# Gate arithmetic for two query chunks at a time in a fused attention and expert kernel

## The chip, the cores and the metric

The kernel runs on one core of one Trainium2 chip. The metric is the device time of one execution in microseconds (us). A core has five engines with queues of their own: TensorE (PE, matmul; its weight loads are PEld), VectorE (DVE), ScalarE (ACT), GpSimd (POOL) and SyncE (SP, which here only issues loads). Each runs its instructions in the order of the program and stops at an instruction whose input is not ready.

## The reference, cut to what matters

```python
# attention: B=4, N=11456, C=128, 49 agents
agent_v = softmax(scale * agents @ k.T) @ v
x = softmax(scale * q @ agents.T) @ agent_v          # (4*11456, 128)
# mixture of experts: 8 experts, D=128, F=1024
do_compute = x @ w_skip > 0
logits = x[do_compute] @ w_gate
e_idx = argmax(logits, axis=1)
gate_w = softmax(logits)[e_idx]
y = gate_w * (relu(x @ w1[e_idx]) @ w2[e_idx])
out = x;  out[do_compute] += y
```

## The kernel before, in words

A batch of 11456 tokens is 90 columns of 128 tokens (the last column is half full). Columns are taken in chunks of 6, so a batch is 15 chunks (`ci` 0 to 14) and the run has 60 of them (n = 15 b + ci). The program is written out in 101 slots. In each slot a table, `ORDER`, names the stages, and each stage takes the chunk that is its lag behind. A stage's name is its letter and its step: k for keys (`sK` scores, `kS` store and running maximum), v for values (`vS` shift, `vE` exp, `vA` product), q and the rest for queries (`sQ` scores, `qS` maximum, `qE` exp, `qT` transpose, `mX` product with the agents' values and the gate matrix, `qN` division, `qD` gate weight, `qG` gate exp, `qO` output). The order in which they are named is the order on every engine:

```python
"kvq": "qN+4 qD+5 sQ+1 bg vE qS+1 sK qE+1 vS-1 qG+4 kS qT+2 bg rt vA qO+5 mX+3 rt wt"
"vq": "qN+4 qD+5 sQ+1 bg vE qS+1 qE+1 vS-1 qG+4 bg qT+2 rt vA qO+5 mX+3 rt wt"
"q": "qN+4 qD+5 sQ+1 qS+1 qE+1 qG+4 bg qT+2 rt qO+5 rt mX+3 rt wt"
```

Keys, values and queries all flow in the slots from 33 to 59 (kvq), values and queries in 60 to 77 (vq), queries alone after that (q). Below, a slot is named by the chunk that `qN` divides in it: "slot n16" begins with the division of chunk 16, whose first instruction is L438 on DVE. So kvq covers n0 to n23, vq n24 to n41, q n42 to n59.

`qN` (L433) reads the product in PSUM (`px`, a single buffer, so the next `mX` waits until both L446 divisions are done), writes the output rows `xs` and the nine gate numbers `G` (eight logits and the skip score), and takes the maximum of the logits, `top` (L460). `qG` subtracts it on POOL (L467) and takes the exp on ACT (L469). `qD`, a slot later, sums (L475) and inverts (L476), which gives the gate weight, and `qO` sends the chunk out from the ACT queue.

Two words move work that belongs to no chunk. `rt` takes one step, up to the next `yield`, of the oldest generator in a queue. These are `codes` (L486: the index of the winning expert, for four chunks at a time, from `G == top`, and its one-hot `mask`), `ranks` (L532) and `routing` (L543), which turn the masks of a batch into each token's place in its expert's list. `mask` and its running counts `cum` come in two parts, of 72 columns (part 0) and 18 columns (part 1). Part 0's place is mask*cum, summed over experts (`sel`, L541), plus mask*start, summed over experts (`acc`, L598), added at L613. `bg` steps the rest: `agent_values` and `early` (L643), which finds the tokens of the first two expert blocks while attention still runs.

When the attention is over, `experts` runs blocks of 384 tokens through w1 and w2, with queues written by hand; the change leaves it as it is.

Of the kernel before, what the change touches and what calls it, by code (L numbers as in the profile page):

```python
# [52 lines left out]
PAR = dict(v=3, q=-1, cols=6, ld=8, more=5, qe=3, eT=2, xs=3, tail=3, early=-8,  # L53
# [74 lines left out]
def attention(nc, tc, sh, io, ps):  # L128
# [10 lines left out]
    with ExitStack() as ctx:  # L139
# [346 lines left out]
        def codes(first, last):  # L486
# [6 lines left out]
            hot = dict(out=best, in0=g[:, :, :NE], in1=top[:, first:last].unsqueeze(2).to_broadcast([P, m, NE]),  # L493
                       op=ALU.is_equal)
            order = dict(out=best, in0=best, in1=desc.unsqueeze(1).to_broadcast([P, m, NE]), op=ALU.mult)
            found = dict(out=mask[i][:, :, first - i * NA_ : last - i * NA_],
                         in0=c.unsqueeze(1).to_broadcast([P, NE, m]),
                         in1=cidx.unsqueeze(2).to_broadcast([P, NE, m]), op=ALU.is_equal)
            if i == 0:
                vec.tensor_tensor(**hot)  # L500
                pool.tensor_tensor(**order)
                yield
                vec.tensor_reduce(c, best, axis=AX.X, op=ALU.max)
                yield
                vec.scalar_tensor_tensor(out=c, in0=g[:, :, NE], scalar=0.0, in1=c, op0=ALU.is_gt, op1=ALU.mult)
                vec.tensor_tensor(**found)
            else:
                vec.tensor_tensor(**hot)
                vec.tensor_tensor(**order)
                vec.tensor_reduce(c, best, axis=AX.X, op=ALU.max)  # L510
                yield
                vec.scalar_tensor_tensor(out=c, in0=g[:, :, NE], scalar=0.0, in1=c, op0=ALU.is_gt, op1=ALU.mult)
                vec.tensor_tensor(**found)
# [29 lines left out]
        def routing(b):  # L543
# [644 lines left out]
```

## Time and profile before

| | |
|---|---|
| median of 3 runs | 786.96 us (785.77 to 787.64) |
| profiled execution: its time, its span | 788.92 us, 787.2 us |
| busy over the span: PE, PEld, DVE, ACT, POOL | 708.2 (90%), 665.6 (85%), 513.3 (65%), 377.2 (48%), 384.1 us (49%) |
| mean granted clock of TensorE | 0.954 of full speed |
| attention ends, first expert matmul begins | 384.4 us, 386.9 us |

The span runs from the first instruction to the last; the time has 1.7 us more around it. Busy times are sums over engines that work side by side, so they add up to more than the span. What limits the kernel changes from stretch to stretch, and the shares above are means over all of them.

### The profile page before, as it was taken

What the parts mean: (1) busy time and instruction counts of PE and PEld (TensorE: products, weight loads), DVE (VectorE), ACT (ScalarE), POOL (GpSimd) and SP (SyncE); (2) the same over time, 40 slices, a digit from 0 to 9 for tenths busy, and PEclk for the clock granted to TensorE, in tenths of its full rate; (3) what the DMA queues carried; (4) which work ended last, traced back from release to release, by engine and by line L of the source; (5) the groups of instructions that cost most, each with busy time, mean ns of one, the idle gap of its engine ahead of it and who ended that gap; (6) DMA issues with size and microseconds to landing.
All of it is one profiled execution on the core that took longest, in us unless ns stands there. A gap on an engine that the chain in (4) does not pass through costs nothing. (4 is left out here: it accounts for less than half of the span.)

```text
span 787.2 us, 18201 instructions
## 1 busy us (share of the span) xinstructions
PE 708.2 (90%) x5542; PEld 665.6 (85%) x5542; DVE 513.3 (65%) x1776; ACT 377.2 (48%) x1076; POOL 384.1 (49%) x482
## 2 busy tenths in 40 slices
PE   6999999989798878884399969999999999999994
PEld 6988999878677767774399969999999999999994
DVE  3424456675667878977667656766767767777663
ACT  3444554444334535553155535555555555555552
POOL 4554233232323251441366663666666666666665
PEclk9999999999889989897599999999999999999998
DMA  9999899988679837653111110111111111111110
GB/s 317 393 387 372 265 371 347 329 263 300 238 223 294 270 101 255 234 183 123 30 36 46 39 30 21 36 49 48 46 49 49 46 51 45 45 47 47 49 28 20
DMA packets 65673, 120.47 MB, mean 153 GB/s; under 512 B 21126, under 2 KB 29322, under 8 KB 65616
## 3 DMA queue, kind: packets, MB, share of 16 engines
q1 hardware_dynamic: 48192, 81.34, 31.6%
q10 hardware_dynamic: 9456, 23.89, 7.7%
q0 software_dynamic: 7968, 14.54, 6.6%
q8 instruction: 29, 0.48, 0.2%
q14 instruction: 28, 0.23, 0.1%
HBM read 87.78 MB, written 31.90 MB: 152 GB/s over the span
## 5 line engine op out<-in xcount | busy, mean ns | idle before, releaser
L946 DVE SCALAR_TENSOR_TENSOR hl<-h,hh 128x384 fp32r<-128x384 f32 x320 | 165.1, 551 | 72.8 <-DVEq L835 72.8
L1008 ACT ACTIVATE hh<-h 128x384 fp32r<-128x384 f32 x320 | 157.1, 492 | 115.1 <-ACTq L835 110.0
L1036 POOL DMA_INDIRECT xg<-out_dram,ids x123 | 125.8, 1023 | 110.1 <-issue 109.8
L409 ACT ACTIVATE qe<-ps_s,qm 128x49 f32<-128x49 f32 x360 | 76.1, 312 | 151.4 <-DVE qm L403 151.4
L1049 POOL DMA_INDIRECT out_dram<-xo,sid x123 | 122.6, 997 | 37.5 <-issue 36.9
L1107 PE MATMUL h<-xh,w 128*128 128x384 f32 x512 | 132.1, 340 | 7.5 <-PEq L835 7.5
L1113 PE MATMUL y<-hh,w 128*128 128x384 f32 x512 | 135.9, 347 | 0.0
L316 PE MATMUL ps_s<-agT,ld 128*128 128x128 f32 x960 | 128.9, 291 | 6.3 <-ACT agT L168 6.3
L316 PEld LDWEIGHTS ps_s<-agT,ld 128*128 128x128 f32 x960 | 118.1, 201 | 17.1 <-ACT agT L168 6.3
L1107 PEld LDWEIGHTS h<-xh,w 128*128 128x128 f32 x512 | 93.2, 190 | 8.2 <-issue 8.1
L1113 PEld LDWEIGHTS y<-hh,w 128*128 128x128 f32 x512 | 88.5, 188 | 1.3 <-issue 0.2
L1107 PE MATMUL h<-xl,w 128*128 128x384 f32 x256 | 86.8, 339 | 0.0
L1113 PE MATMUL y<-hl,w 128*128 128x384 f32 x256 | 86.3, 337 | 0.0
L332 DVE TENSOR_TENSOR run<-scores,run 128x294 f32<-128x294 f32 x56 | 28.7, 513 | 85.0 <-ACT scores L327 83.2
L430 PE MATMUL ps_x<-av,eT 50*128 50x138 f32 x720 | 62.4, 307 | 19.6 <-DVE G L446 16.8
L467 POOL TENSOR_TENSOR ex<-G,top 128x48 f32<-128x48 f32 x60 | 16.3, 271 | 125.1 <-DVE gs L475 68.8
L430 PEld LDWEIGHTS ps_x<-av,eT 50*128 50x128 f32 x720 | 49.9, 196 | 31.4 <-issue 22.0
L316 PE MATMUL ps_s<-agT,lds 128*128 128x128 f32 x480 | 65.1, 292 | 0.0
L316 PEld LDWEIGHTS ps_s<-agT,lds 128*128 128x128 f32 x480 | 60.2, 203 | 5.6 <-issue 3.9
L446 DVE TENSOR_TENSOR xs<-ps_x,qr 128x768 f32<-128x768 f32 x60 | 57.5, 959 | 6.5 <-DMA out_dram<-xs 4.3
L1004 ACT ACTIVATE yT<-y 128x384 f32<-128x384 f32 x40 | 19.7, 492 | 65.3 <-ACTq L835 65.3
L920 DVE SCALAR_TENSOR_TENSOR junk<-id,rs,jot 128x90 f32<-128x90 f32 x120 | 31.1, 308 | 28.0 <-DVEq L835 28.0
(193 smaller groups left out, 1168.7 us busy)
## 6 DMA issues: line engine op xcount, KB each, us to landing
out_dram<-xs ACTq DMA_DIRECT2D x60, 387.0 KB, 4.7
ld<-in_q_dram SPq DMA_DIRECT2D x44, 384.0 KB, 4.7
ld<-in_v_dram SPq DMA_DIRECT2D x38, 387.0 KB, 5.6
ld<-in_k_dram SPq DMA_DIRECT2D x36, 384.0 KB, 5.7
lds<-in_k_dram SPq DMA_DIRECT2D x24, 384.0 KB, 6.3
lds<-in_v_dram SPq DMA_DIRECT2D x22, 387.0 KB, 5.3
ld<-in_moe_w_dram SPq DMA_DIRECT2D x24, 256.0 KB, 5.6
lds<-in_q_dram SPq DMA_DIRECT2D x16, 384.0 KB, 5.6
```

Source lines behind the costliest of these rows:

```text
L316: r.append(ten.matmul(pt[:, t * NA : t * NA + P], lhsT=xT[:, t * P : (t + 1) * P], rhs=agT[:, b, :], start=True, stop=True))
L332: vec.tensor_tensor(out=run, in0=stored(n), in1=run, op=ALU.max)
L409: act.activation(qes[n % PAR["qe"]][:, t, :NA], s[:, t, :], AF.Exp, bias=mx[:, t : t + 1])
L430: ten.matmul(px[:, h, t, :], lhsT=eT[s, t * P : (t + 1) * P], rhs=st["av", b][s, :], start=True, stop=True)
L446: vec.tensor_tensor(out=out[:r, h, j, :], in0=px[:r, h, j, w], op=ALU.mult, in1=rs[:r, h, j].unsqueeze(3).to_broadcast(list(px[:r, h, j, w ...
L920: w = v.scalar_tensor_tensor(out=junk[:, h, :], in0=id_ps[:, h, : sh.NC], scalar=rs[:, 1 + h : 2 + h], in1=ps.jot, op0=ALU.is_equal, op1=A ...
L946: v.scalar_tensor_tensor(out=hl[:, f], in0=h_ps[f % HB], scalar=0.0, in1=hh[:, f], op0=ALU.max, op1=ALU.subtract).then_inc(sem["HL"], 1)
L1008: s.activation(hh[:, f], h_ps[f % HB], AF.Relu).then_inc(sem["HH"], 1)
L1036: g.indirect_dma_start(out=xg[n % TURN][:, h, :], out_offset=None, in_=out, in_offset=bass.IndirectOffsetOnAxis(ap=ids[:, n % TURN, h : h ...
L1049: g.indirect_dma_start(out=out, out_offset=bass.IndirectOffsetOnAxis(ap=sid[:, n % 2, h : h + 1], axis=0), in_=xo[:, n % 2, h, :], in_offs ...
L1107: w = t.matmul(h_ps[f % HB], lhsT=ps.w1[e][wx][:, cs], rhs=x, start=(n == 0), stop=(n == 2))
L1113: w = t.matmul(y_ps, lhsT=ps.w2[e][wx][:, f, :], rhs=h[:, f], start=(f == 0 and n == 0), stop=(f == FC - 1 and n == 2))
```

## The change

For pairs of chunks (0 and 1, 2 and 3, up to 12 and 13, and 14 alone) the maximum, the subtraction, the exp, the sum and the reciprocal are each one instruction over 12 columns. They are issued in the slot of the pair's second chunk, the sum and the reciprocal a slot later, and the maximum stands behind `qS` and no longer in `qN`. The maximum is subtracted in `G` itself. The weight is copied by POOL into the two chunks' `xs`, and both chunks go out together, a slot later for the first. `xs` has four buffers for three. `codes` finds the winner as `G >= 0`, in one instruction with the weighting that POOL (part 0) or DVE (part 1) did. For batches 0 to 2, part 0 of the places becomes mask*(cum + start) with one sum over experts. `routing` has more `yield`s ahead of its matmuls and of that sum. `early` has two more, and its one-hot shares the room of `routing`'s table `r1`.

```diff
-PAR = dict(v=3, q=-1, cols=6, ld=8, more=5, qe=3, eT=2, xs=3, tail=3, early=-8,
+PAR = dict(v=3, q=-1, cols=6, ld=8, more=5, qe=3, eT=2, xs=4, tail=3, early=-8,
...
-            vec.tensor_reduce(top[:, at : at + m], G[:, at : at + m, :NE], axis=AX.X, op=ALU.max)
+        def couple(n):
+
+            b, ci, cols, m = geometry(n)
+            if ci % 2 == 0 and ci < NCH - 1:
+                return (), 0, 0
+            both = (n - 1, n) if ci % 2 else (n,)
+            return both, sh.AT[ci + 1 - len(both)], sh.AT[ci + 1]
 
         def query_gate(n):
...
+            g = G[:, first:last, :NE]
+            top = wk.tile([P, 2 * M], F32, name="top")[:, : last - first]
+            vec.tensor_reduce(top, g, axis=AX.X, op=ALU.max)
+            pool.tensor_tensor(out=g, in0=g, in1=top.unsqueeze(2).to_broadcast(g.shape), op=ALU.subtract)
+            act.activation(exs[n // 2 % 2][:, : last - first, :NE], g, AF.Exp)
...
+            gs = wk.tile([P, 2, 2 * M], F32, name="gs")[:, :, : last - first]
+            vec.tensor_reduce(gs[:, 0, :], exs[n // 2 % 2][:, : last - first, :], axis=AX.X, op=ALU.add)
+            vec.reciprocal(gs[:, 1, :], gs[:, 0, :])
+            for i in both:
+                at = sh.AT[chunks[i][1]] - first
+                pool.tensor_copy(st["xs", i][:, :, C], gs[:, 1, at : at + geometry(i)[3]])
 
         def query_out(n):
-            b, ci, cols, m = geometry(n)
-            act.dma_start(out=sh.chunk(out, b, cols), in_=st.pop(("xs", n)))
+            for i in couple(n)[0]:
+                act.dma_start(out=sh.chunk(out, *chunks_cols(i)), in_=st.pop(("xs", i)))
...
+            vec.scalar_tensor_tensor(out=best, in0=g[:, :, :NE], scalar=0.0, in1=desc.unsqueeze(1).to_broadcast([P, m, NE]),
+                                     op0=ALU.is_ge, op1=ALU.mult)
...
-        def ranks():
+        def ranks(last):
 
             yield from count(0)
             cum = part[0][0]
+            if not last:
+                return
             yield
             pool.tensor_tensor(out=cum, in0=cum, in1=mask[0], op=ALU.mult)
...
-                pool.tensor_tensor(**product)
+                pool.tensor_tensor(out=big, in0=big, in1=starts0, op=ALU.add)
+                pool.tensor_tensor(out=big, in0=big, in1=mask[0], op=ALU.mult)
...
             if not last:
-                v.tensor_reduce(acc, big.rearrange("p e j -> p j e"), axis=AX.X, op=ALU.add)
+                yield
+                with nc.allow_low_precision("exact integers"):
+                    v.tensor_reduce(rki[:, :NA_], big.rearrange("p e j -> p j e"), axis=AX.X, op=ALU.add)
...
-            v.tensor_tensor(out=rki[:, :NA_], in0=acc, in1=sel, op=ALU.add)
+            if last:
+                v.tensor_tensor(out=rki[:, :NA_], in0=acc, in1=part["sel"], op=ALU.add)
...
             if not last:
                 yield
+                yield
             pd = ps_e.tile([P, 512], F32, name="ps_e")
...
-                hit = rt.tile([P, TB], BF16, name="ehit")
+                hit = rt.tile([P, sh.KB * NE], F32, name="r1").bitcast(BF16)[:, :TB]
                 vec.tensor_scalar(hit, ps.iota, rec[:, 0:1], None, op0=ALU.is_ge)
+                yield
+                yield
                 yield
```

DVE, slot n16 (kvq, an odd chunk of its batch), in the kernel before, with the `rt` step of that slot behind L332:

```order
L438 RECIPROCAL qr<-ps_x 128x6
L446 TENSOR_TENSOR xs<-ps_x,qr 128x2x3x128
L446 TENSOR_TENSOR G<-ps_x,qr 128x2x3x9
L460 TENSOR_REDUCE top<-G 128x6
L475 TENSOR_REDUCE gs<-ex_200 128x6
L476 RECIPROCAL xs<-gs 128x6
L403 TENSOR_REDUCE qm<-ps_s 128x6
L332 TENSOR_TENSOR run<-scores,run 128x294
L508 TENSOR_TENSOR best<-G,top 128x96
L509 TENSOR_TENSOR best<-best,desc 128x96
L510 TENSOR_REDUCE code<-best 128x12
L512 SCALAR_TENSOR_TENSOR code<-G,code 128x12
```

The same slot in the changed kernel (its L405 is L403 of before, L477 the new maximum; line numbers behind the first edits are higher):

```order
L440 RECIPROCAL qr<-ps_x 128x6
L448 TENSOR_TENSOR xs<-ps_x,qr 128x2x3x128
L448 TENSOR_TENSOR G<-ps_x,qr 128x2x3x9
L405 TENSOR_REDUCE qm<-ps_s 128x6
L477 TENSOR_REDUCE top<-G 128x12
L334 TENSOR_TENSOR run<-scores,run 128x294
L508 SCALAR_TENSOR_TENSOR best<-G,desc 128x48
L512 TENSOR_REDUCE code<-best 128x6
L514 SCALAR_TENSOR_TENSOR code<-G,code 128x6
L515 TENSOR_TENSOR mask_205<-code,cidx 128x8x6
```

Three small instructions left the stretch between the division and `qm`; in the even slots L487 and L488, over 12 columns, stand there in their place. The `rt` work has come forward by a step or two, since `ranks` has two steps fewer.

DVE, behind L332 of slots n19 and n20, the routing of batch 0, before:

```order
L573 TENSOR_TENSOR a_2260<-start,oin_1862 128x8
L574 TENSOR_TENSOR a_2261<-start,n_1865 128x8
L575 TENSOR_TENSOR a_2261<-a_2261,oin_2130 128x8
L577 TENSOR_TENSOR ds<-start 128x8
L585 CAST cnt<-bi 128x1
L598 TENSOR_REDUCE acc<-cum_1846 128x72
```

This is all that slot n20 has behind L332. In the changed kernel the first five (L580 to L593 there) stand in slot n19, behind the eight that slot has in both kernels (L559 to L569, then L566 to L576), and slot n20 has this between its maximum and the next division:

```order
L405 TENSOR_REDUCE qm<-ps_s 128x6
L477 TENSOR_REDUCE top<-G 128x12
L334 TENSOR_TENSOR run<-scores,run 128x294
L608 TENSOR_REDUCE rki<-cum_1819 128x72
L440 RECIPROCAL qr<-ps_x 128x6
```

PE, the end of batch 0's routing (slots n22 and n23), where L626 needs `twob`, DVE's last result of slot n22; before:

```order
L430 MATMUL ps_x<-av_170,eT 128x138 x6
L626 LDWEIGHTS diff
L626 MATMUL ps_e<-twob,diff 128x180
L316 MATMUL ps_s<-agT,ld_93 128x128 x6
L316 MATMUL ps_s<-agT,lds 128x128 x6
L417 MATMUL ps_e<-ident,qe_104 128x128 x3
```

and in the changed kernel (L638 is L626 of before):

```order
L432 MATMUL ps_x<-av_170,eT 128x138 x6
L318 MATMUL ps_s<-agT,ld_93 128x128 x6
L318 MATMUL ps_s<-agT,lds 128x128 x6
L419 MATMUL ps_e<-ident,qe_104 128x128 x3
L638 LDWEIGHTS diff
L638 MATMUL ps_e<-twob,diff 128x180
```

The twelve score matmuls of the next slot and the three transposes now stand ahead of the matmul that needs `twob`.

## Rows read from the trace of the kernel before

**Rows 1.** Busy time of each engine in five stretches: the stretch and its length, then busy us of PE, PEld, DVE, ACT and POOL (and how many instructions), the granted TensorE clock, the share of the DMA engines that was busy and GB/s.

```profile
60.00:128.00 68.00, 67.95 (x699) 60.98 (x696) 33.52 (x98) 35.37 (x132) 23.36 (x33) 1.00 0.95 339
...
156.00:219.00 63.00, 53.31 (x505) 48.14 (x504) 41.82 (x129) 26.50 (x104) 19.41 (x30) 0.92 0.80 265
219.00:303.00 84.00, 72.79 (x726) 62.18 (x724) 64.34 (x221) 37.05 (x159) 27.58 (x50) 0.92 0.72 230
303.00:362.00 59.00, 48.38 (x431) 42.32 (x429) 50.34 (x173) 31.39 (x131) 20.41 (x34) 0.94 0.60 207
...
391.00:787.00 396.00, 376.98 (x2389) 370.58 (x2387) 265.46 (x960) 207.02 (x437) 247.59 (x246) 0.98 0.16 41
```

**Rows 2.** Waits between 128 and 391 us: who waited for whom, us in total, times, longest.

```profile
ACT qe L409 <- DVE qm L403: 125.0, 48, 4.6
...
PE ps_x L430 <- DVE G L446: 16.8, 15, 3.0
...
PE ps_e L626 <- DVE twob L622: 11.9, 3, 6.5
```

**Rows 3.** DVE in order of time in slot n16 (kvq): start, duration, line, operation, out<-in, idle before and what ended it.

```profile
168.77 0.19 DVE L438 RECIPROCAL qr<-ps_x 128x6 f32<-128x6 f32 x1
...
169.87 0.20 DVE L446 TENSOR_TENSOR G<-ps_x,qr 128x54 f32<-128x54 f32 x1
170.11 0.20 DVE L460 TENSOR_REDUCE top<-G 128x6 f32<-128x48 f32 x1
170.23 0.20 DVE L475 TENSOR_REDUCE gs<-ex 128x6 f32<-128x54 f32 x1
170.46 0.19 DVE L476 RECIPROCAL xs<-gs 128x6 f32<-128x6 f32 x1
170.57 0.42 DVE L403 TENSOR_REDUCE qm<-ps_s 128x6 f32<-128x294 f32 x1
172.75 0.47 DVE L332 TENSOR_TENSOR run<-scores,run 128x294 f32<-128x294 f32 x1 [1.76 <-ACT scores L327]
173.13 0.25 DVE L508 TENSOR_TENSOR best<-G,top 128x96 bf16<-128x96 f32 x1
...
173.95 1.04 DVE L512 SCALAR_TENSOR_TENSOR code<-G,code 128x12 f32<-128x12 f32 x1
...
175.70 0.18 DVE L438 RECIPROCAL qr<-ps_x 128x6 f32<-128x6 f32 x1
```

**Rows 4.** ACT in the same slot.

```profile
171.03 0.30 ACT L409 ACTIVATE qe<-ps_s,qm 128x49 f32<-128x49 f32 x1 [3.12 <-DVE qm L403]
...
172.15 0.28 ACT L469 ACTIVATE ex<-ex 128x48 f32<-128x48 f32 x1
172.28 0.44 ACT L327 COPY scores<-ps_s 128x294 f32<-128x294 f32 x1
```

**Rows 5.** The columns of rows 1, for slots cut from the xs division of a chunk to that of a later one: n2 (kvq, no `rt` work), n14 and n15, n16, n18, n19 to n23, n34 to n37, n41 (vq), n43 to n46, n47 to n50, n56 (q, no `rt` work).

```profile
93.57:98.48 4.91, 4.91 (x54) 4.42 (x53) 2.59 (x8) 2.88 (x11) 0.47 (x2) 1.00 0.57 193
155.93:169.00 13.07, 11.26 (x103) 10.11 (x102) 9.21 (x24) 5.36 (x21) 5.04 (x6) 0.87 0.87 279
169.00:175.92 6.92, 6.92 (x77) 6.25 (x75) 4.92 (x14) 2.94 (x11) 2.24 (x3) 1.00 0.83 262
181.30:187.46 6.16, 5.10 (x56) 4.66 (x55) 4.17 (x13) 2.94 (x11) 1.74 (x3) 1.00 0.84 289
187.46:219.12 31.66, 25.82 (x240) 23.43 (x240) 20.30 (x68) 12.85 (x51) 9.44 (x18) 0.89 0.74 247
264.38:287.30 22.92, 15.95 (x168) 13.38 (x166) 18.70 (x71) 9.18 (x39) 8.67 (x15) 0.93 0.56 184
299.87:303.44 3.57, 3.57 (x42) 3.08 (x41) 3.11 (x12) 2.11 (x10) 0.27 (x1) 1.00 0.90 296
307.29:324.17 16.88, 13.25 (x112) 11.53 (x111) 15.31 (x55) 7.53 (x33) 5.03 (x7) 0.90 0.53 177
324.17:342.44 18.27, 14.53 (x124) 12.90 (x123) 16.85 (x55) 10.07 (x40) 9.93 (x15) 0.91 0.71 238
...
357.66:360.43 2.77, 2.68 (x28) 2.25 (x26) 2.12 (x8) 1.92 (x10) 0.27 (x1) 1.00 0.36 143
```

**Rows 6.** DVE's groups by line and shape between 80 and 391 us: how many, busy us in total, mean ns of one, idle us just before them.

```profile
L500 DVE TENSOR_TENSOR best<-G,top 128x192 bf16<-128x192 f32 x12 | 4.2, 349 | 0.0
...
L598 DVE TENSOR_REDUCE acc<-cum 128x72 f32<-128x576 f32 x3 | 3.6, 1195 | 0.0
...
L613 DVE TENSOR_TENSOR rki<-acc,sel 128x72 int32<-128x72 f32 x4 | 3.1, 780 | 0.0
...
L661 DVE SCALAR_TENSOR_TENSOR ejunk<-ps_s,rec,jot 128x90 f32<-128x90 f32 x6 | 1.8, 296 | 0.1
```

**Rows 7.** POOL's groups, as rows 6.

```profile
L467 POOL TENSOR_TENSOR ex<-G,top 128x48 f32<-128x48 f32 x60 | 16.3, 271 | 125.1 <-DVE gs L475 68.8 <-DVE top L460 56.3
...
L537 POOL TENSOR_TENSOR cum<-cum,mask 128x576 f32<-128x576 f32 x4 | 5.1, 1274 | 0.0
```

**Rows 8.** POOL's L584 and DVE's L577, which started behind it, in slot n20, and DVE's L577 of the last batch, whose POOL was idle.

```profile
197.50 1.15 POOL L584 TENSOR_TENSOR cum<-mask,a 128x576 f32<-128x576 bf16 x1 [2.84 <-DVE a L574]
...
197.55 1.12 DVE L577 TENSOR_TENSOR ds<-start 128x8 f32<-128x8 f32 x1
...
377.42 0.16 DVE L577 TENSOR_TENSOR ds<-start 128x8 f32<-128x8 f32 x1
```

More of the change, by code (lines that the diff above doesn't have):

```diff
@@ L232, in attention @@
         nc.vector.memset(G[sh.LAST :, sh.NC - 1, :], -1.0)
-        top = one.tile([P, sh.NC], F32, name="top")
-        exs = [const.tile([P, M, NE + 1], F32, name=f"ex{i}") for i in range(3)]
+        exs = [const.tile([P, 2 * M, NE + 1], F32, name=f"ex{i}") for i in range(2)]
         for x in exs:
@@ new lines, in query_gate @@
+        def query_gate(n):
+            both, first, last = couple(n)
+            if not both:
+                return
[4 more added lines that the diff above has]
+            act.activation(exs[n // 2 % 2][:, : last - first, :NE], g, AF.Exp)
+        def query_weight(n):
+            both, first, last = couple(n)
+            if not both:
+                return
+            gs = wk.tile([P, 2, 2 * M], F32, name="gs")[:, :, : last - first]
[4 more added lines that the diff above has]
+                pool.tensor_copy(st["xs", i][:, :, C], gs[:, 1, at : at + geometry(i)[3]])
@@ L492, in codes @@
             best = rt.tile([P, 24, NE], BF16, name="best")[:, :m, :]
[L493 to L498, printed above, removed]
+            vec.scalar_tensor_tensor(out=best, in0=g[:, :, :NE], scalar=0.0, in1=desc.unsqueeze(1).to_broadcast([P, m, NE]),
+                                     op0=ALU.is_ge, op1=ALU.mult)
             if i == 0:
-                vec.tensor_tensor(**hot)
-                pool.tensor_tensor(**order)
                 yield
[L503 to L513, printed above, removed]
+            vec.tensor_reduce(c, best, axis=AX.X, op=ALU.max)
+            yield
+            vec.scalar_tensor_tensor(out=c, in0=g[:, :, NE], scalar=0.0, in1=c, op0=ALU.is_gt, op1=ALU.mult)
+            vec.tensor_tensor(out=mask[i][:, :, first - i * NA_ : last - i * NA_],
+                              in0=c.unsqueeze(1).to_broadcast([P, NE, m]),
+                              in1=cidx.unsqueeze(2).to_broadcast([P, NE, m]), op=ALU.is_equal)
         part = {}
@@ L578, in routing @@
             rki = rt.tile([P, NC], I32, name="rki")
-            big, sel = part[0][0], part["sel"]
-            product = dict(out=big, in0=mask[0], in1=a[0].unsqueeze(2).to_broadcast([P, NE, NA_]), op=ALU.mult)
+            big = part[0][0]
+            starts0 = a[0].unsqueeze(2).to_broadcast([P, NE, NA_])
             if last:
-                v.tensor_tensor(**product)
+                v.tensor_tensor(out=big, in0=mask[0], in1=starts0, op=ALU.mult)
             else:
-                pool.tensor_tensor(**product)
+                pool.tensor_tensor(out=big, in0=big, in1=starts0, op=ALU.add)
+                pool.tensor_tensor(out=big, in0=big, in1=mask[0], op=ALU.mult)
             v.tensor_copy(cnt[:, NE:], bi[:, NE : NE + 1])
@@ L754, in out_done @@
             if ci == NCH - 1 - PAR["tail"]:
-                queue.append(ranks())
+                queue.append(ranks(b == sh.B - 1))
             if ci == NCH - 1:
@@ L797, in attention @@
                 step(back)
+            early_x()
             while len(queue) > 1:
-                step(queue, 1)
-            step(queue, 1)
-            early_x()
+                step(queue, len(queue) - 1)
             while queue:
```

15 lines of the change are left out of this document (5 added, 10 removed).

## The prediction

> **What bounds the kernel now.** I read the busy times by stretch first, since the shares of the whole span mix stages. From 391 us on the experts run with PE busy for 377 of 396 us; the change does not touch them [rows 1]. Only the 390 us ahead of them can move. From 60 to 128 us PE is busy for 67.95 of 68 us at full clock: work taken off DVE is worth nothing there. After 156 us PE has holes: 53.3 of 63, 72.8 of 84 and 48.4 of 59 us, at a mean granted clock of 0.92 to 0.94, while DVE rises to 50 of 59 us [rows 1]. Of the waits in that part, the longest is ACT's for `qm`, a result of DVE, and PE waits 16.8 us for DVE to empty the product buffer [rows 2].
>
> Next I followed one slot through. In n16 DVE takes 1.80 us from L438 to the start of `qm` (168.77 to 170.57). ACT starts its six exps when `qm` is done (171.03), reaches the gate exp at 172.15 and the copy of the key scores at 172.28; DVE's L332 waits for that copy until 172.75, and only at 173.13 does the `rt` work start. The next L438 follows it, at 175.70 [rows 3, 4]. So a kvq slot is a loop through DVE and ACT of 4.36 us (173.13 - 168.77) plus the `rt` work R. PE needs 4.91 us for such a slot (n2, the first row of [rows 5]). R up to about 0.55 us is free, and what lies above it makes the slot longer; n16 has R = 2.57 and lasts 6.92 us. In vq and q the loop has no key copy: DVE's own 2.2 us (1.80 and `qm`) plus R stand against PE's 3.57 and 2.77 us (n41 and n56 in [rows 5]). The slots with heavy R are those near the end of each batch, where codes, ranks and routing run; each also leaves PE idle, and a stretch at half clock often follows (n14 and n15 have a mean clock of 0.87, n19 to n23 of 0.89) [rows 5].
>
> **The loop's own part.** Between the start of the G division and `qm` DVE spends 0.70 us on the division and three small instructions (169.87 to 170.57) [rows 3]. In an odd slot all three are gone; `qm` follows the division by the 0.24 us after which L460 did, so 0.46 us are saved. In an even slot the sum and the reciprocal remain, over 12 columns. The trace has no such reduce; it lies between 0.20 us (L475, 54 elements) and 0.35 us (L500, 192 elements) [rows 3, 6]. I take 0.25, near the first, since the length grows little with size: with L460's step of 0.12 us gone, 0.07 us are saved, between nothing and 0.12. On ACT an even slot has no gate exp, a step of 0.13 us; an odd one has an exp twice as long, at most 0.13 us more, and I take 0.05 [rows 4]. So 0.41 us in an odd and 0.20 us in an even slot, 0.3 us on average, wherever the loop decides.
>
> [...]
>
> What is hidden: the maximum over 12 columns stands behind `qm`, beside ACT's six exps (171.03 to 172.15). It needs about 0.25 us on DVE and a POOL subtraction of 0.27 to 0.54 us (L467, once to twice) [rows 4, 7], so some 0.3 us of cover are left; without it the gate exp, and behind it the score copy, `eT` and the next `rt` work, come late by what is missing. The POOL copies of the weights (no such row; at most L467's 0.27 us each) lie between the reciprocal at about 1.7 us of a slot and the output at its end: they cost nothing unless POOL is 2 us behind. The fourth `xs` buffer holds a pair together; the first chunk's landing has as much time as before, so I put that at 0 (half a us either way).
>
> **The `rt` part.** For batches 0 to 2 DVE loses L598 and L541, two sums of one shape and 1.2 us each, and gets one such sum back; L613 (0.78 us) goes; POOL loses L501 and runs two passes over 576 elements (1.15 and 1.27 us) back to back, for two apart [rows 6, 7, 8]. [...] L577 takes 0.16 us with POOL idle and 1.12 us started behind L584 [rows 8]; L512 took 1.04 us in n16 [rows 3]. Now L577's successor starts behind the first of two passes, in one step with the eight instructions ahead.
>
> [...]
>
> **Slot by slot**, against the floors: kvq. n14 and n15: 0.3 us each. n16: R falls from 2.57 to four instructions over 6 columns, some 0.85 us, so PE's 4.91 decides: 2.0. n17: 0.2. n18: its step is now empty, 6.16 to 4.91: 1.25. n19 to n23 (31.66 us): n19 takes over L573 to L585, 1.12 us for L577 and some 0.1 for each of the other four: 1.5 lost; n20 has one sum of 1.2 us left, 4.36 - 0.41 + 1.2 = 5.1 where it had 4.36 + 1.5 + 1.2 = 7.1: 1.9; n21 loses L613, but the next two-input instruction takes over its stall: 0.4; n22: POOL has routing's four passes, the weights and a shift ahead of the gate's subtraction, which comes about 1 us late: 0.2 lost; n23: the twelve score matmuls no longer stand behind `twob` (5.4 us of PE's wait in rows 2 is n22 and n37, the rest the last batch): 2.0. Sum: 2.0 + 1.25 + 0.8 - 1.5 + 1.9 + 0.4 - 0.2 + 2.0 = 6.6.
>
> vq. n34 to n37 take 22.9 us, 4.2 of them idle on DVE [rows 5]. They lose L613 (0.8), 4 x 0.3 of the loop, and half of `early`'s selection, three of L661 and three smaller ones, some 1.5 us, which goes to n39; of the idle time I count half, 2.2, since PE no longer stops there for `early` and `twob` with the next slot's scores behind; and 1.3 us come on in n37, where the one-hot of `early` waits for POOL's passes over `r1` to leave the room they share. Sum 4.4. n38, whose matmuls stood behind `twob`: 1.4. n39 takes `early`'s last part, half of it in its slack: 0.7 lost. Three other DVE-bound slots, 0.2 each. Sum 5.7.
>
> q. n43 to n46, 16.9 us, DVE busy for 15.3 of them [rows 5]: without L541 (1.2), two of L509, as short as L460 (0.2 each), and 0.3 a slot, 14.1: 2.8. n47 to n50, 18.3 us: L613, 4 x 0.3, and 1.0 of DVE's idle 1.4 us, in part waits for POOL: 3.0. n51 to n58: waits for POOL's L501 go: 0.5. Sum 6.3.
>
> The last batch keeps its two sums and its steps; the last gate subtraction now stands ahead of L537 on POOL (0.35 us) and two small DVE instructions go (0.4): 0. `early_x` is written earlier, but the queue is empty by then, so its instructions stay where they were.
>
> Together 18.6 us. These slots have PE as their second bound, and half-clock stretches behind every stall that remains, so I count a little under four fifths: 14.5 us. From the profiled 788.92 us that is 774.4; the median of the runs is 1.96 us lower, so the prediction is 773 us, its own range 768 to 778.
>
> **Rivals.** *PE absorbs it* (780 us): the slots close up only until PE's half-clock stretches decide, and a third to a half of the 18.6 us comes through. For it: PE is at 100% with clock 1.00 in n16 itself [rows 5]. Against it: its instructions there were queued work of a slot of 4.9 us, not of 6.9. *More than the sum* (765 us): with the holes the half-clock stretches go too. Clock 0.92 over 63 and 84 us and 0.94 over 59 [rows 1] is 5.0 + 6.7 + 3.5 = 15 us of lost clock, of which half would be 7.5. *No change* (787 us): the kernel is held by the DMA there. The share is 0.95 up to 128 us, but 0.72 to 0.80 where the holes are [rows 1], so this needs the outputs in pairs to collide with the loads. *Slower* (793 us): the gate's subtraction on POOL comes late in every odd slot, as I expect for n22. At 1 us each, 30 odd slots cost 30 us against the whole sum of 18.6 and some 5 us of slack below the floors, so some 6 us more than before. It decides from 23.6 / 30 = 0.8 us on average; POOL is busy only 19 of 63 and 28 of 84 us [rows 1], which speaks against it.
>
> **How the numbers follow.** Forecast 0.5, PE absorbs it 0.22, more than the sum 0.12, no change 0.07, slower 0.09. Faster by over 0.2% (1.6 us, about what a measurement of this kernel can tell) 0.84, within it 0.07, slower 0.09. The range goes from 764, just below the second rival, up to 785, which leaves out no change, slower and a little of the rest; the unknown 12-column reduce (0.1 us in 30 slots) and the two passes' stalls (3.6 us) lie inside.
>
> **What would show it.** L438 of n17 and of n19 each 4.9 us behind the one before it; no wait of PE for `twob` in batches 0 and 1; n20 near 5.1 us; PE busy above 57 of the stretch that n14 to n23 take; the first expert matmul near 372 us; the same 400 us behind it. Wrong: waits of ACT's gate exp for POOL in most odd slots, waits of DVE for the landing of `xs`, L577 and its successors over 2 us together, or half-clock stretches as many as before.

## The result and the profile after

The changed kernel takes 764.0 us (median of 4 runs, 762.23 to 766.18) where the kernel before takes 787.3 us on the same chip (4 runs, 785.77 to 789.39): a ratio of 0.970 [0.967, 0.974], 23.3 us less. The forecast was 773 us with a range of 764 to 785: the direction was right, the size was not, and the time lies on the range's lower end (763.995 us before rounding).

Nearly all of it lies ahead of the experts. The profiled execution took 762.23 us, its span is 760.4 us; the first expert matmul begins at 361.22 us where it began at 386.9, and 399.2 us follow it where 400.3 did. Chunk 59's division, the last of the attention, starts at 342.29 us for 367.94, 25.65 us earlier; from there to the first expert matmul nothing changed (18.9 and 19.0 us). The two profiled executions lie 26.7 us apart and the medians 23.3, so sums over slots come out some 3 us above the gain in time.

Busy time by stretch of the changed kernel, columns as in [rows 1]; the third to fifth rows are n14 to n23 (kvq), n24 to n41 (vq) and n42 to n58 (q):

```profile
60.00:128.00 68.00, 67.96 (x699) 61.11 (x699) 32.36 (x86) 34.55 (x126) 23.94 (x36) 1.00 0.97 338
128.00:153.83 25.83, 25.83 (x269) 23.48 (x269) 16.29 (x49) 13.01 (x50) 7.07 (x13) 1.00 0.95 333
153.83:209.59 55.76, 50.81 (x522) 45.13 (x520) 36.10 (x111) 25.92 (x99) 21.44 (x38) 1.00 0.92 314
209.59:283.00 73.41, 67.92 (x723) 58.08 (x724) 59.69 (x192) 36.88 (x152) 26.97 (x53) 0.98 0.77 261
283.00:342.29 59.29, 48.86 (x442) 42.85 (x441) 50.62 (x159) 31.34 (x125) 20.72 (x41) 0.93 0.62 213
```

The same work took 72.17 us up to n14 (now 70.60), 63.19 us in kvq, 84.32 in vq and 64.50 in q [rows 1, 5]. PE is now busy for 91%, 93% and 82% of the three stages, and the granted clock is 1.00, 0.98 and 0.93 in them, where it was 0.92, 0.92 and 0.94. Its waits between 128 and 391 us:

```profile
ACT qe L411 <- DVE qm L405: 96.7, 47, 4.2
...
ACT ex L479 <- POOL G L478: 10.4, 5, 4.2
...
PE ps_x L432 <- DVE G L448: 9.7, 12, 1.9
...
PE ps_e L638 <- DVE twob L633: 7.5, 3, 6.5
...
DVE xs L448 <- DMA out_dram<-xs: 5.0, 6, 1.7
```

Against [rows 2]: ACT waits 28 us less for `qm`, PE 7 us less for the product buffer, and of the waits for `twob` the last batch's 6.5 us and 1.0 us in two others are left. DVE's waits for landings of outputs have not become shorter: 5.0 us, for 3.9 before. DVE in slot n16 (L448 the division, L477 the new maximum over 12 columns):

```profile
165.57 0.19 DVE L440 RECIPROCAL qr<-ps_x 128x6 f32<-128x6 f32 x1
165.85 0.96 DVE L448 TENSOR_TENSOR xs<-ps_x,qr 128x768 f32<-128x768 f32 x1
166.73 0.20 DVE L448 TENSOR_TENSOR G<-ps_x,qr 128x54 f32<-128x54 f32 x1
166.85 0.45 DVE L405 TENSOR_REDUCE qm<-ps_s 128x6 f32<-128x294 f32 x1
167.22 0.24 DVE L477 TENSOR_REDUCE top<-G 128x12 f32<-128x96 f32 x1
```

`qm` starts 0.12 us behind the start of G's division; before it was 0.70 us [rows 3]. And the slots of [rows 5] that the forecast spoke of, n14 with n15, n16, n18, n19, n20, n22, n23, n34 to n37, n38:

```profile
153.83:165.85 12.02, 11.83 (x122) 10.81 (x121) 8.25 (x25) 5.31 (x20) 4.73 (x8) 1.00 0.96 307
165.85:171.53 5.68, 5.59 (x61) 4.89 (x60) 3.84 (x11) 2.97 (x11) 1.64 (x2) 1.00 0.92 357
176.43:180.60 4.17, 4.17 (x50) 3.68 (x49) 2.18 (x6) 2.68 (x11) 0.35 (x1) 1.00 0.91 329
180.60:187.43 6.83, 6.83 (x76) 6.13 (x74) 4.83 (x21) 2.57 (x10) 3.69 (x6) 1.00 1.00 327
187.43:192.45 5.02, 4.01 (x42) 3.69 (x39) 3.28 (x8) 2.45 (x10) 2.05 (x3) 1.00 1.03 414
197.97:204.09 6.12, 5.00 (x52) 4.36 (x48) 3.21 (x11) 2.56 (x10) 3.38 (x7) 1.00 0.61 216
204.09:209.59 5.50, 3.71 (x38) 2.95 (x37) 3.64 (x12) 2.28 (x9) 1.74 (x4) 1.00 1.00 356
251.45:268.43 16.98, 15.08 (x171) 12.98 (x170) 15.92 (x54) 7.50 (x33) 8.75 (x17) 1.00 0.60 216
268.43:271.34 2.91, 2.61 (x31) 1.91 (x30) 2.24 (x8) 1.80 (x9) 1.33 (x4) 1.00 0.19 19
```

### The profile page after: what moved, and what is told of

It reads as the page before. It is cut to its first block, busy times and chain, and to the rows that moved or that the text cites. A ratio compares the mean times of both kernels' runs of the same rounds, so it can differ in the third digit from the quotient of the medians.

```text
span 760.4 us, 18157 instructions
## 1 busy us (share of the span) xinstructions
PE 696.2 (92%) x5542; PEld 655.7 (86%) x5542; DVE 495.6 (65%) x1677; ACT 374.8 (49%) x1048; POOL 383.7 (50%) x502
## 5 line engine op out<-in xcount | busy, mean ns | idle before, releaser
L318 PE MATMUL ps_s<-agT,ld 128*128 128x128 f32 x960 | 126.0, 287 | 6.2 <-ACT agT L168 6.2
L318 PEld LDWEIGHTS ps_s<-agT,ld 128*128 128x128 f32 x960 | 115.3, 197 | 13.9 <-ACT agT L168 6.2
L432 PE MATMUL ps_x<-av,eT 50*128 50x138 f32 x720 | 60.2, 299 | 13.1 <-DVE G L448 9.7
L432 PEld LDWEIGHTS ps_x<-av,eT 50*128 50x128 f32 x720 | 48.3, 190 | 24.8 <-issue 17.8
L448 DVE TENSOR_TENSOR xs<-ps_x,qr 128x768 f32<-128x768 f32 x60 | 57.5, 959 | 8.2 <-DMA out_dram<-xs 5.0
L318 PE MATMUL ps_s<-agT,lds 128*128 128x128 f32 x480 | 60.8, 280 | 0.0
L318 PEld LDWEIGHTS ps_s<-agT,lds 128*128 128x128 f32 x480 | 56.0, 192 | 3.0 <-issue 0.7
L491 POOL COPY xs<-gs 128x6 f32<-128x6 f32 x60 | 10.3, 202 | 82.3 <-issue 50.2
```

The costliest lines, as they stand in the source:

```text
L318: r.append(ten.matmul(pt[:, t * NA : t * NA + P], lhsT=xT[:, t * P : (t + 1) * P], rhs=agT[:, b, :], start=True, stop=True))
L432: ten.matmul(px[:, h, t, :], lhsT=eT[s, t * P : (t + 1) * P], rhs=st["av", b][s, :], start=True, stop=True)
L448: vec.tensor_tensor(out=out[:r, h, j, :], in0=px[:r, h, j, w], op=ALU.mult, in1=rs[:r, h, j].unsqueeze(3).to_broadcast(list(px[:r, h, j, w ...
```

## The experiments

Some of the chips take 896 to 899 us for the kernel before, in place of 785 to 787: on them PE waits for its own sequencer in the expert part (62.7 us at L1115 of `early_only`; the same line in the kernel before, L1113, has no wait). So each ratio is to the kernel before on its own chip; the last column, the start of chunk 59's division in the profile, lies ahead of that part and can be read across chips, to a few us only: `early_only`, as fast as the kernel before, has 365.83 for its 367.94, and the one program of the last row scatters by 6 us.

| run | ratio to before [95%] | before there, us | chunk 59 at, us |
|---|---|---|---|
| the change | 0.970 [0.967, 0.974] | 787.3 | 342.29 |
| `after_again` | 0.978 [0.975, 0.981] | 895.9 | 342.88 |
| `single`, `single_again` | 0.969 [0.965, 0.973], 0.970 [0.967, 0.973] | 785.2, 786.7 | 342.32, 342.70 |
| `oldroute` | 0.982 [0.979, 0.985] | 785.2 | 349.82 |
| `newroute_oe` | 0.992 [0.988, 0.995] | 785.2 | 359.54 |
| `warm` | 1.000 [0.998, 1.003] | 785.2 | 365.50 |
| `s_topfirst` | 0.986 [0.982, 0.990] | 898.5 | 350.36 |
| `s_codespool` | 0.979 [0.975, 0.983] | 898.5 | 344.40 |
| `s_earlyold` | 0.979 [0.975, 0.982] | 898.5 | 344.13 |
| `s_xs3` | 0.984 [0.981, 0.988] | 898.5 | 349.19 |
| `s_shift` | 0.971 [0.968, 0.974] | 786.7 | 341.72 |
| `early_xs4` | 0.992 [0.990, 0.995] | 786.7 | 359.31 |
| `early_only` | 0.999 [0.997, 1.002] | 896.2 | 365.83 |
| `gate_only` | 0.989 [0.986, 0.992] | 786.7 | 352.79 |
| `s_pdyield` | 0.981 [0.977, 0.985] | 896.2 | 344.98 |
| `s_sumlast`, `_again`, `_third` | 0.975 [0.970, 0.979], 0.975 [0.972, 0.978], 0.968 [0.964, 0.972] | 896.2, 895.9, 787.4 | 336.46, 342.59, 339.48 |

**Which part pays: pairs, routing, gates.** The changed kernel with one chunk at a time:

```diff
-            if ci % 2 == 0 and ci < NCH - 1:
-                return (), 0, 0
-            both = (n - 1, n) if ci % 2 else (n,)
+            both = (n,)
```

> The changed kernel with its gate steps one chunk at a time again (still subtracted in place, sent out chunk by chunk). If the small instructions ahead of qm are a main part of the gain, 0.3 us in each of some 35 slots that DVE decides come back: 772 to 775 us. If the gain is that of the routing steps alone, it stays at 764 to 766 us.

> The changed kernel with the gate steps for one chunk at a time, again, as the partner of the three runs beside it. Every theory: ratio to the kernel before near 0.97 on this chip, with the division of chunk 59 near 342.3 us.

`single` is as fast as the change: pairing adds nothing to the time. The next two put the old `ranks` and `routing` into the changed kernel (`oldroute`) and the new ones alone into the kernel before (`newroute_oe`).

> The changed kernel with the ranks and the routing of before (two sums over experts, the products apart, the matmuls one step earlier); gates in pairs, codes and early as changed. By the slot sums of the prediction the routing part is worth 10 to 12 us: 774 to 777 us. If the pairs carry the gain, 766 to 769 us.

> The kernel before with the ranks and the routing of the changed one, and nothing else. If the parts add up, 787 less what oldroute gives back: 774 to 778 us. If the routing needs the shorter gate steps to be of use, 780 us or more.

Routing is worth 1.2% taken out of the change and 0.8% added to the kernel before: 6 to 9 us, and not the 10 to 12 of the slot sums. `gate_only` is the kernel before with the gates and codes of `single` and with `early`'s steps.

> The kernel before with the gate steps and the codes of the changed one, for one chunk at a time (maximum behind qm, subtracted in G, weight copied by POOL) and with early's new steps; ranks, routing and the three xs buffers as before. If the parts add up (routing 6 to 7 us, fourth buffer 5 us, of 24.5 in all): 11 to 13 us faster than before, ratio 0.984 to 0.986. If the fourth buffer pays only with the new routing: 16 to 18 us faster, ratio 0.978. If the maximum's place is worth only what stands behind it in the forecast's sum, 0.1 to 0.4 us in the slots that the loop decides: 5 to 8 us, ratio 0.990 to 0.994.

The gates give 1.1%, 8.4 us, between the ranges of the first and the third theory. With routing (0.8%) and the fourth buffer (0.8%, below) that is 2.7 of the 3.0% that `single` gains: the parts add up within their intervals.

**Why the gates pay: what stands ahead of `qm`.** `s_topfirst` is `single` with the maximum back in the division, `s_codespool` has the codes in two steps again, `s_shift` moves routing's eight instructions behind the count from n19 to n18.

> The kernel of single with each chunk's maximum back inside the division stage, ahead of qm. If what stands ahead of qm decides the slots, 0.12 to 0.24 us come back in each of some 35 slots: 765 to 769 us against single's 761. If not, 760 to 763 us.

> The kernel of single with the winner's index in two steps again, the comparison on DVE and the weighting on POOL (part 0) or DVE (part 1). In the kernel before DVE stood about 0.7 us for POOL at 12 such places and L509 cost 0.2 us at 8: 3 to 7 us if these stalls come through, 764 to 768 us; under 763 us if they fall beside other waits.

> The single-chunk form with one empty step fewer ahead of routing's count matmul and one more ahead of its sum, so that the eight instructions behind the count fall into slot n18 and the five behind them stay in n19; all later steps stay where they were. Theory that VectorE and ScalarE's loop decides a slot once its added work is over 0.55 us, with a slot of 4.9 us of PE work as the floor: n18 goes from 4.1 to 4.9, n19 from 6.9 to near 5.8, so 0.3 us in each of batches 0 to 2, up to 0.5; in all 0.5 to 1.5 us faster than the single-chunk form. Theory that a batch's added work counts by its sum, wherever it stands (slots lend time to each other through the buffers): the same within 0.5 us.

The maximum's place alone costs 0.7 to 0.8%: 884.21 us beside 878.42 and 878.28 for `s_codespool` and `s_earlyold` on the same chip, 0.986 beside 0.978 for the change on another such chip. Each of n15 to n20 is 0.30 to 0.32 us longer than in `single`, as the maximum puts 0.31 us ahead of `qm` there, and the slots up to n14 take 72.15 us again. The codes' form makes no difference that shows, and `s_shift` is no faster: in batch 0 n18 took over what n19 lost and more (11.02 us together, now 11.98), and in batch 1 n33 and n34 became shorter (8.26 us, now 7.46). In n18 the fourth of the moved instructions (L567; the same one, L568 there, takes 0.17 us in `single_again`, with POOL idle) stood behind a POOL pass and ended with it (182.32 and 182.29 us); DVE and POOL of `s_shift`, in order of time:

```profile
180.86 0.17 DVE L565 TENSOR_SCALAR nb<-nb 128x8 int32<-128x8 int32 x1
181.07 1.25 DVE L567 TENSOR_SCALAR cnt<-nb 128x8 int32<-128x8 int32 x1
```

```profile
181.02 1.27 POOL L308 TENSOR_TENSOR w<-ld,w 128x512 fp32r<-128x512 f32 x1 [1.77 <-ACT w L307]
```

`s_sumlast` tests the same cause by going on: the gate weight's sum and reciprocal leave the stretch ahead of `qm` too.

```diff
-    "q": "qN+4 qD+5 sQ+1 qS+1 qE+1 qG+4 bg qT+2 rt qO+5 rt mX+3 rt wt",
+    "q": "qN+4 sQ+1 qS+1 qE+1 qG+4 qD+5 bg qT+2 rt qO+5 rt mX+3 rt wt",
```

(and alike for the other two).

> The single-chunk form with the gate weight's sum and reciprocal, too, moved from ahead of qm to behind the maximum and POOL's subtraction, in every slot. Theory that each instruction ahead of qm lengthens every slot that the loop through VectorE and ScalarE decides, and one behind it does not: 0.35 us (two steps of 0.24 and 0.11) leave that stretch in some 30 slots, so 4 to 8 us faster than the single-chunk form, ratio to the kernel before 0.960 to 0.965. Theory that the maximum's move paid through something else (the codes, POOL's part): the same as the single-chunk form, ratio 0.968 to 0.972. Theory that TensorE has become the bound: the same too, with TensorE's idle time unchanged.

> The single-chunk form with the gate weight's sum and reciprocal behind the maximum, again, beside the changed kernel itself. If the 6 us by which the division of chunk 59 came earlier in its first run are real: 4 to 7 us faster than the changed kernel on this chip. If they are given back behind the attention: within 2 us of it.

> The changed kernel, as the partner of the run beside it. Every theory: the division of chunk 59 at 342.3 us, ratio to the kernel before near 0.970 where the kernel before takes 785 to 787 us.

In all three runs n15 to n21 and n23 are 0.29 to 0.40 us shorter each than in `single`, 2.3 us over n14 to n23. So VectorE and ScalarE's loop still decides there. The time gains less than the 4 to 8 us of that theory: 874.97 us beside 876.25 for the change on one chip, whose intervals overlap, and 761.8 us (0.968) on another. That this version beats the change is likely, not shown.

**The fourth buffer.** `s_xs3` takes it from `single`; `early_xs4` gives it, with `early`'s steps, to the kernel before; `early_only` is those steps alone, `s_earlyold` is `single` without them.

> The kernel of single with three buffers for the output rows, as before. DVE waited 4.3 us in all for landings before and 5.0 after the change; a fourth buffer gives single a whole slot more. If that is part of the gain, 763 to 766 us; if the waits come only where the loads are slow anyway, 760 to 762 us.

> The kernel before with the new steps and the shared room of early, and four xs buffers for three; gates, codes, ranks and routing as before. If the fourth buffer frees the division from the landing of outputs in any order of work (the 4.3 us of waits for landings that the kernel before has): 3 to 5 us faster than before, ratio 0.994 to 0.996. If it pays only in the changed kernel, whose slots are shorter, so that an output has less time to land: 0 to 1 us, ratio 0.999 to 1.001, and the waits for landings that vanish come back as waits for PE or ScalarE.

> The kernel before with the new steps and the shared room of early alone, three xs buffers. If the fourth buffer made the 6 us that both together gave: 0 to 1 us faster than before, ratio 0.999 to 1.001. If early's steps made them: 5 to 6 us, ratio near 0.993. If it was half and half, as the slots tell (n24, n25 and n30 2.6 us, the slots of early 3.2 us): near 0.996.

> The kernel of single with one step between the one-hot of early and its matmuls, as before, where the change has three. If PE's stops for that one-hot (4.5 us in two places before) are a part that I undercounted in n34 to n38, 764 to 766 us; if they were hidden or the spread only moves them, 760 to 762 us.

`early`'s steps are worth nothing that shows in the time, and the buffer 0.6 to 0.8%, 5 to 6 us, in the kernel before as in the single-chunk form. What it is worth to pairs was not run. DVE in slot n30 of `s_xs3`:

```profile
245.95 0.96 DVE L448 TENSOR_TENSOR xs<-ps_x,qr 128x768 f32<-128x768 f32 x1 [1.95 <-DMA out_dram<-xs]
```

In `single` this division starts without a wait, and the slot takes 3.46 us for 5.39. The waits for landings are 5.6 us in `s_xs3` and 4.8 in `early_only`; `early_xs4`, whose attention is 6.5 us shorter than that of `early_only`, has one of 0.27 us left.

**PE behind `twob`.** `s_pdyield` puts the matmul that needs `twob` ahead of the next slot's scores again.

> The single-chunk form with one step fewer between twob and the matmul that needs it, as in the kernel before: the twelve score matmuls stand behind that matmul again. Theory of the forecast (2.0 us in n23 and 1.4 us in n38 come from this move): 2.5 to 4 us slower than the single-chunk form, ratio to the kernel before near 0.974, with TensorE's wait for twob back in batches 0 and 1. Theory that routing's gain is the sums that VectorE lost, and that a batch's scores are far enough ahead: within 1 us of the single-chunk form, ratio 0.970.

n23 and n38 are longer by 1.8 and 1.2 us, near the forecast's 2.0 and 1.4. But n24 is 1.5 us shorter than in `single`: there PE waits for something else. PE of the changed kernel, then of `s_pdyield`, at the end of the last keys (`mx` and `gmr`, the maximum over them):

```profile
208.91 0.28 PE L341 MATMUL ps_e<-ident,mx 128*49 128x128 f32 x1 [1.08 <-DVE mx L338]
211.26 0.39 PE L348 MATMUL ps_e<-ident,gmr 49*128 49x49 f32 x2 [2.07 <-DVE gmr L345]
```

```profile
204.37 0.24 PE L635 MATMUL ps_e<-twob,diff 128*128 128x180 bf16 x1 [3.70 <-DVE twob L631]
...
212.35 0.27 PE L341 MATMUL ps_e<-ident,mx 128*49 128x128 f32 x1
213.62 0.42 PE L348 MATMUL ps_e<-ident,gmr 49*128 49x49 f32 x2 [1.00 <-DVE gmr L345]
```

With the wait for `twob` gone, PE reaches the keys' maximum 3.15 us too early; with it, 1.00 us. So n23's gain is given back one slot later, and from the first division to n44's `s_pdyield` takes 207.45 us where `single` and `single_again` take 207.82 and 207.55. That chunk 59 still comes 2.3 to 2.7 us later stems from n44 on: n45 lasts 5.19 us (4.32 and 3.77 in the two), n49 5.34 (4.69 and 4.68) and n50 4.63 (2.52 and 2.54). PE's four waits for `twob` are 13.6 us, of which n23 has 3.70 and the longest 6.5; what stretched n44 to n50 is not shown. In the time the matmul's place shows as 0.3% (0.981 beside 0.978), within the intervals.

**What half clock costs.** `warm` is the kernel before with 16 small matmuls ahead of the product of 20 chunks, to keep PE busy; they add to no result. Half clock is the lower of the two levels that TensorE's granted clock has in the trace: of 1140 windows of 0.2 us from 128 to 356 us in the kernel before, 979 read 1.00 and 146 read 0.50 (n25: 0.50 up to 229.55 us, 1.00 from 230.05), so a slot's clock of 0.69 is a mean of both.

> The kernel before with 16 small bf16 matmuls, whose result nobody reads, in front of the product of 20 chunks at whose place PE was idle. They change no wait. If the half-clock stretches behind the holes are themselves a large part of the cost (some 31 us at half speed, 15 us of clock, of which PE's own share would be 6 to 10), the clock of the attention rises and the time falls to 777 to 782 us. If the clock only follows the waits on DVE and costs little, 786 to 790 us.

The same slots in the kernel before and in `warm` (n15, n21, n25, n48):

```profile
163.46:169.00 5.54, 4.31 (x28) 4.09 (x29) 3.61 (x10) 2.42 (x10) 2.23 (x3) 0.69 0.93 288
200.02:205.98 5.96, 4.74 (x31) 4.63 (x32) 4.10 (x12) 2.94 (x11) 1.47 (x3) 0.71 0.56 205
225.55:231.46 5.91, 5.91 (x43) 5.24 (x43) 2.87 (x9) 2.12 (x9) 1.47 (x3) 0.64 0.49 147
330.33:335.63 5.30, 4.07 (x26) 3.85 (x27) 5.06 (x15) 2.28 (x9) 2.80 (x7) 0.68 0.72 265
```

```profile
162.93:168.46 5.53, 5.53 (x65) 4.94 (x63) 3.61 (x9) 2.42 (x10) 2.23 (x3) 1.00 0.92 268
199.46:205.42 5.96, 5.28 (x61) 4.82 (x58) 4.10 (x13) 2.93 (x11) 1.47 (x3) 1.00 0.59 215
226.51:230.28 3.77, 3.77 (x44) 3.28 (x43) 2.75 (x10) 1.74 (x9) 1.47 (x3) 1.00 0.39 109
328.31:333.60 5.29, 3.06 (x31) 2.58 (x29) 5.05 (x15) 2.28 (x9) 2.79 (x7) 1.00 0.75 271
```

At full clock n15, n21 and n48 are as long as at 0.68 to 0.71: DVE decides them. Where PE is busy throughout at the lower clock, n25 gains 2.1 us and n38 1.6 us. This is n38, before and in `warm`:

```profile
287.30:292.73 5.43, 5.43 (x43) 4.77 (x43) 2.76 (x9) 2.12 (x9) 3.04 (x5) 0.69 0.26 82
```

```profile
287.14:290.97 3.83, 3.83 (x43) 3.35 (x43) 2.67 (x9) 1.77 (x9) 1.84 (x3) 1.00 0.24 86
```

The fillers took as much elsewhere (n24 is 1.5 us longer, n27 and n34 1.0 us each). In the faster kernels the clock shows in more slots. `s_sumlast` and `s_sumlast_again` are one program; n44 with n45, and n46 to n51, in each:

```profile
287.51:294.58 7.07, 4.77 (x46) 4.22 (x46) 6.46 (x27) 3.61 (x17) 2.14 (x5) 1.00 0.47 142
294.58:316.36 21.78, 17.37 (x171) 15.35 (x170) 20.75 (x73) 14.09 (x56) 14.82 (x25) 1.00 0.77 265
```

```profile
288.33:298.20 9.87, 7.54 (x43) 6.66 (x43) 6.54 (x26) 4.30 (x18) 2.12 (x5) 0.65 0.45 152
298.20:322.20 24.00, 20.29 (x170) 18.09 (x169) 20.78 (x72) 13.79 (x55) 14.77 (x25) 0.86 0.72 253
```

n24 and n25 lose another 1.4 us, and every other slot agrees within 0.3 us. The time at half clock is taken as twice the missing share: 2 x (0.35 x 9.87 + 0.14 x 24.00) = 13.6 us in `s_sumlast_again`, whose slots are 5.0 us longer. The third run was to tell whether that holds again.

> The single-chunk form with sum and reciprocal behind the maximum, a third time. In its two runs the slots up to n23 agree to 0.1 us and are 0.3 us each shorter than in the single-chunk form, but in one of them four stretches at half clock stand in n24, n44, n49 and n51, and these slots are 6.1 us longer together. If the stretches at half clock make the whole difference: the division of chunk 59 at 336.5 us plus 0.35 us for each us at half clock above 7, whatever the chip. If it is something else of that chip: the attention is 336 to 337 us long here with half-clock stretches as well, or 342 without them.

It has n44 and n45 at a clock of 0.80 (8.67 us) and n46 to n51 at 1.00 (21.78 us): 3.5 us at half clock, 1.6 us longer. So in these slots a us at half clock went with 0.37 to 0.46 us more. Over all slots the three runs have 6.6, 13.8 and 24.3 us at half clock, and by the sum in the expectation 13.8 gives 338.9 us for the 339.48 that came, of which 0.60 is a wait for a landing. The changed kernel's own two runs differ in q too: it takes 59.29 us at a clock of 0.93, and 57.14 us in `after_again`, where its clock is not shown. The kvq and vq slots are 0.6 and 1.4 us longer there, so chunk 59 comes no earlier.

## Why the prediction was right and wrong

**Right: the loop, and kvq as a whole.** n16 gained 1.2 us (forecast 2.0), n18 2.0 (1.25), n19 lost 1.3 (1.5), n20 gained 2.0 (1.9) and lasts 5.02 (5.1), n22 lost 0.3 (0.2), n23 gained 1.85 (2.0), n14 and n15 1.05 (0.6). In kvq 7.4 came of 6.6, by some luck: n16 and n18 miss by 0.8 the one way and 0.75 the other. The price of POOL's first pass was right too: in each of three batches one DVE instruction (L582) takes 1.14 us behind it, for 0.17 in the last batch, which has no such pass. POOL and DVE in n19 and n20 of the changed kernel:

```profile
185.98 1.15 POOL L591 TENSOR_TENSOR cum<-cum,a 128x576 f32<-128x576 f32 x1 [2.69 <-DVE a L581]
187.20 1.27 POOL L592 TENSOR_TENSOR cum<-cum,mask 128x576 f32<-128x576 f32 x1
```

```profile
186.01 1.14 DVE L582 TENSOR_TENSOR a<-a,oin 128x8 f32<-128x8 f32 x1
...
187.43 0.96 DVE L448 TENSOR_TENSOR xs<-ps_x,qr 128x768 f32<-128x768 f32 x1
```

The division beside the second pass takes the 0.96 us that it takes elsewhere. That both passes stop an instruction, the 3.6 us in the forecast's range, is shown by no run: the first stopped L582 alone, and the second none. Nor does a run show as a rule that the next two-input instruction takes over L613's stall, on which n21's 0.4 rests: in n21 DVE's L625 took 0.83 us beside a POOL instruction (L613 of the changed kernel, 196.83 to 197.67 us) where its like before (L614) took 0.29, and the slot gained 0.44 us. The 12-column reduces take 0.24 and 0.25 us, as taken.

**Wrong: the discount to four fifths.** This step and the sum for vq are what failed. "These slots have PE as their second bound" does not hold in kvq: n18 lasts 4.17 us, and 3.81 in `s_sumlast`, below the 4.91 us taken as PE's floor. A slot is cut at DVE's division, and PE's 4.9 us of work spreads over its neighbours, so the floor holds for a stage (50.8 of 55.8 us), not for a slot. In vq PE is busy for 93%, but only behind a gain of 10.9 us. And the "half-clock stretches behind every stall that remains" did not eat the gain: fewer are left than before (11.2 us at half clock for 30.6, below), and n25 gained 2.05 us as its own went (clock 0.64, now 1.00). Without the discount the sum is 18.6; the attention gave 25.65 in the profiled executions, 7.4 in kvq for 6.6, 10.9 in vq for 5.7, 5.2 in q for 6.3 and 2.1 ahead of n14, where 0.5 lies ahead of the first division.

**The fourth buffer at 0: it came out, but the buffer's worth was missed.** The working had "the first chunk's landing has as much time as before", and DVE does wait for landings as long as before, 5.0 us in the changed kernel for

```profile
DVE xs L446 <- DMA out_dram<-xs: 3.9, 7, 1.4
```

So no part of the miss is such a wait that went. But that asked what the pair takes from the buffer, not what a fourth one gives: where each chunk goes out by itself, `s_xs3` and `early_xs4` put it at 5 to 6 us. The change spends this on sending two outputs at once; no run has pairs with three buffers, so that is argued from the waits.

**Wrong: nothing ahead of n14.** The 67.95 of 68 us were read up to 128 us, and the sum went on at n14, at 156. Between, n8 to n13 are slots that the loop decides: 1.6 us came there. In `single` it is 1.35, all of it the maximum's place, as `s_topfirst` takes it back whole. PE was as busy there as ahead of it, so the step that failed is the reading of a busy share near 100% as a bound; the kernel before:

```profile
128.00:156.00 28.00, 27.93 (x283) 25.23 (x282) 17.97 (x60) 13.13 (x52) 9.28 (x15) 1.00 0.95 329
```

**Mis-sized: the loop's own part.** `qm` was to follow the division by the 0.24 us after which L460 did. It follows by 0.12: the 0.24 fits a wait of L460 for its own input, `G` (L476, which reads the result ahead of it, starts 0.23 us behind L475, and L403, which does not, 0.11 us behind L476) [rows 3]. So an odd slot saves 0.58 us and not 0.46 ahead of `qm`, an even one 0.14 (0.07). The step also laid the gain to the pairs. A single chunk saves 0.24 in each slot, and a pair's two outputs at once give the rest back, since DVE waits for landings again (5.0 us in the waits above, none in either run of `single`).

**Mis-sized: vq, 5.7 for 10.9.** n34 to n37 gave 5.9 (4.4) and n38 2.5 (1.4). Of n38's, `s_pdyield` gives 1.2 to the place of the matmul, and by `warm` 1.6 us of its length before was the price of half clock; the two overlap. n24 to n33 gave 3.4 where 0.6 stood: n25 lost its stretch at half clock (2.05), and the sum had no term for batch 1's L541 in n30 (1.2 us, and 1.0 us of waiting for POOL ahead of it), though n30 to n33 gave only 0.6, with a wait of 1.3 us for a landing at the end of n33. In q 5.2 came of 6.3: n43 to n46 gave 0.5 of 2.8, n47 to n50 1.5 of 3.0 (n49 is now 1.9 us longer), n42 and n51 to n58 3.3 of 0.5.

**The rivals.** PE absorbing it is refuted by the size. The time is that of "more than the sum" (765 us), and its reason holds in part: half-clock time fell from 30.6 us (2 x the missing clock of [rows 1]) to 11.2, but by `warm` the kernel before paid for it in few slots, at most 2.1 us in n25, 0.6 in n36 and 1.6 in n38, of the 25.65. The gate's exp waits for POOL 5 times between 128 and 391 us, not in most odd slots, which refutes the slower rival. "No change" is refuted by the size as well.

**The signs.** n17 and n19 did not come 4.9 us behind the slot ahead: n16 takes 5.68, n18 4.17. PE is busy for 50.8 us of n14 to n23, not above 57. Of the waits for `twob` in batches 0 and 1, 0.6 us is left in batch 0. n20 is 5.02, the first expert matmul comes at 361 for 372, and 399 us follow it. Of the signs of being wrong, one came: DVE waits for landings, 5.0 us.

What stays open: 0.3% of the gain, some 2 us, is in none of the three parts alone, which is no more than their intervals. Of vq's miss some 1.5 us in n34 to n37 is not traced to a cause.

## What to carry to other kernels

In a loop through two engines, put behind the instruction that the other engine waits for whatever it does not need: the maximum moved there, 0.31 us, shortened n15 to n20 by 0.30 to 0.32 us each, and merging the same instructions into larger ones gave nothing more (0.970 beside 0.969 for `single`). A busy share near 100% of one engine does not show that another engine's work is hidden: n9 to n13 became 1.3 us shorter together though PE had been busy for 27.93 of 28 us. Price an added buffer by the waits for landings that it takes away (4.8 us in `early_only`, 0.27 in `early_xs4`), and look whether the rest of the change brings them back, as the pairs did (5.0 us). When a wait is taken away, read which result the same engine needs next: PE's wait for `twob` (3.70 us in `s_pdyield`) came back one slot later as one for the keys' maximum (3.15 us for 1.00).

## What the runs showed of the hardware

A stretch at half clock cost nothing where DVE decides the slot (n15: 5.54 and 5.53 us at 0.69 and 1.00) and 0.5 us per us where PE is busy throughout (n25, n38). In n44 to n51 of one program it went with 0.37 to 0.46 us per us, and that program's attention lasted 336.46, 339.48 or 342.59 us as such stretches fell.

A DVE instruction with one input and a constant (L567 of `s_shift`, 8 integers) took 1.25 us behind a POOL pass that had started 0.05 us earlier, and 0.17 us in `single_again` with POOL idle. The forecast, in n21, spoke of a two-input instruction.

The kernel before takes 785 to 787 us on some chips and 896 to 899 on others. The attention is as long on both: chunk 59's division starts at 342.29 and 342.88 us in the changed kernel. PE's groups of the expert part in the changed kernel on a chip of the first and of the second kind (`after_again`):

```profile
L1126 PE MATMUL y<-hh,w 128*128 128x384 f32 x512 | 135.9, 347 | 0.0
```

```profile
L1126 PE MATMUL y<-hh,w 128*128 128x384 f32 x512 | 144.4, 364 | 64.2 <-PEq L848 64.0
```

There PE waits 64 us more for its own sequencer at this line, of the 112 us by which the medians differ. Why those chips do so is open.
